# GpSimd's two-input work in parts of 192 columns, silu's low part on VectorE, and a list transposed one product group later

## The chip, the core and the metric

The kernel runs on one core of a Trainium2 chip. The core has five engines with a queue each: TensorE (PE; its weight loads are shown as PEld), VectorE (DVE), ScalarE (ACT), GpSimd (POOL) and SyncE (SP), which here only starts transfers. Each engine works through its own instructions in the order of the program and waits at semaphores for the others. The metric is the device time of one execution in microseconds, the median of three runs.

## What is computed

Three stages follow each other: attention with a hash mask, a silu MLP over all tokens, and eight experts of which each token uses one or none.

```python
# attention: 2 batches, 8 heads, 768 tokens, 64 columns a head
q_bucket, k_bucket = bits of (q @ proj > 0), (k @ proj > 0)
scores = where(q_bucket == k_bucket, q @ k.T / 8, -1e9)
x = softmax(scores) @ v                          # 1536 tokens x 512
# MLP, 2048 wide
h = x @ w_in
x = (h * sigmoid(h)) @ w_out
# experts: E = 8, each 512 -> 1024 -> 512
do = x @ w_skip > 0
e  = argmax(x[do] @ w_gate);  g = softmax(...)[e]
out = x;  out[do] = x + g * (relu(x @ w1[e]) @ w2[e])
```

## The kernel before

Matmuls take operands rounded to a shorter format (F32R), so nearly every operand is kept in two parts: a high part, the rounded copy, and a low part, the operand less its high part. Three products (high by high, low by high, high by low) then stand for one. In the names, `whi` and `wlo` are the parts of a weight, `gh` and `gl` those of silu's output `g`, `xhi` and `xlo` those of the attention's output, `xTh` and `xTl` those of an expert's transposed tokens. High parts are mostly made by ScalarE's copy, low parts by a subtraction on VectorE or GpSimd.

**Attention** goes over eight head pairs, twelve steps each, 96 in all. A step is one head and 128 query tokens: TensorE makes the scores `S` (line 381), VectorE their maximum `mx` (391) and from it the pair `bs` of scale and bias, two columns wide (393), ScalarE the exponentials `P` (395), TensorE their transposes `T` (407), ScalarE and VectorE copy these to `PT` (410, 412), and TensorE multiplies them by `v` (`pv`, 421). For every six steps the row sums `sums` (six columns) get 1e-9 added and are inverted on VectorE (425, 426), transposed on TensorE (`rT`, 432) and sent through memory to come back as `rb`; `em_x` then has GpSimd multiply `x` by `rb` (453), copy it to `xhi` (454) and subtract to get `xlo` (455). Beside a pair's steps the next pair's operands are made by `prep_op`: on ScalarE `K` (309) and `Q` (312), on GpSimd a copy of `Q` (312), the low part of `K` (316), the low part of `Q` (320), a scaling of `raw` (303) and the mask `mb` (337). The tables `PRE` and `POST` give the step in which each of these is issued.

**The MLP** goes over three blocks of 512 tokens and, in each, over 16 product groups f of 128 hidden columns, n = 0 to 47 in all. `em_h(n)` multiplies by `w_in` (`ph`, line 606, twelve matmuls), ScalarE makes `g` (612) and `gh` (613), and the subtraction for `gl` stands on line 615. TensorE then does `em_out(n - 1)` (`o`, 651 or 642). The MLP's weights come as 64-bit floats and are put together by `convert(f)`: ScalarE scales the upper word into `u` (214), VectorE shifts the lower one into `mag` (215), joins both (219) and writes the weight `wraw` (223). They are split in `splitting` into `whi` (ScalarE, 249) and `wlo` (VectorE, 252). In block 0 the loop over n converts f = n + 2 for n = 2 to 13 and splits n + 1, so a weight is made one group ahead of its use; later blocks find all weights in memory. The loop sets the order on ScalarE: `whi` of n + 1, `u` twice for n + 2, then `g` and `gh` of n.

**The experts** run a plan written as a list: `h` is one piece of the first product (six matmuls, `eh`, 1048), `y` one piece of the second (`ey`, 1070), `x` the transposition of an expert's gathered tokens, `t` that of its hidden values (both `tr`, 1026), `fetch` the gathers for later experts. Tokens per expert come from a list `id_d` that GpSimd scatters to memory (780). Experts 0 and 1 have theirs from a quicker way; the list of the others is read back as `eidr` (1000, a transfer on ScalarE's queue), transposed on TensorE as `eT` (1124) and written to `eid` by VectorE (1125). The start of the plan is

```python
fetch 0; h 0,0,0; h 0,0,1; h 0,1,0; t 0,0; h 0,1,1; y 0,0; y 0,1; x 1; t 0,1
fetch 1; h 1,0,0; h 1,0,1; y 0,2; y 0,3; t 1,0; ...
```

and before the change the transposition `eT` follows `t 0,1`. Behind `eid` stand the gathers for experts 2 and 3. `gT`, the gate weights on their way to memory, is copied on line 991.

Of the kernel before, what the change touches and what calls it, by code (L numbers as in the profile page):

```python
# [9 lines left out]
F32 = mybir.dt.float32  # L10
# [5 lines left out]
ALU = mybir.AluOpType  # L16
# [3 lines left out]
P = 128  # L20
# [5 lines left out]
def kernel(  # L26
# [16 lines left out]
    nc = tc.nc  # L43
    B, H, D, S = qT.shape
    NTOK, DM = out.shape
    NF = mw.shape[0]
# [3 lines left out]
    HQ = S // 2  # L50
# [5 lines left out]
    NT = NTOK // P  # L56
# [51 lines left out]
    xlo = xp.tile([P, KD, NTOK], F32R, name="xlo")  # L108
# [56 lines left out]
    NEARLY, NRING, NMORE = 4, 12, 8  # L165
# [98 lines left out]
    def attention(hook):  # L264
# [31 lines left out]
        def own(hd):  # L296
            return slice(hd * D, (hd + 1) * D)

        def prep_op(i, hd, what, eng):

            ks, qs = raws[i]
            if what == "scale":
                eng.tensor_scalar(ks, ks, SC, None, op0=ALU.mult)
                return
            Q1, K1, Q2, K2 = ops[i]
            r, o = own(hd), own(1 - hd)
            if what in ("kh", "k2"):
                dst = K1[r, hd] if what == "kh" else K2[0:D, hd]
                nc.scalar.activation(dst, ks[r], AF.Copy, scale=1.0 if i else SC)  # L309
            elif what in ("qa", "qb"):  # L310
                dst = Q1[r if what == "qa" else o, hd]
                (nc.scalar.copy if eng is nc.scalar else eng.tensor_copy)(dst, qs[r])
            elif what == "kl":
                h = K1[r, hd].bitcast(F32)
                if i:
                    eng.tensor_tensor(K1[o, hd], ks[r], h, op=ALU.subtract)
                else:
                    eng.scalar_tensor_tensor(K1[o, hd], ks[r], SC, h, op0=ALU.mult, op1=ALU.subtract)
            else:
                eng.tensor_tensor(Q2[0:D, hd], qs[r], Q1[r, hd].bitcast(F32), op=ALU.subtract)  # L320

        def prep_proj(i):

# [124 lines left out]
        def em_x(u, x, rb, eng):  # L448
            i, qh = units[u]
            b, p = divmod(i, NP)  # L450
            t0 = b * S + qh * HQ
            hi = xhi[:, p, t0:t0 + HQ]
            eng.tensor_tensor(x, x, rb, op=ALU.mult)
            eng.tensor_copy(hi, x)
            eng.tensor_tensor(xlo[:, p, t0:t0 + HQ], x, hi.bitcast(F32), op=ALU.subtract)


        mxs = [mainp.tile([P, 2], F32, name=f"mx{j}", bufs=1) for j in range(4)]
# [18 lines left out]
        Q1, K1, Q2, K2 = ops[0]  # L477
# [12 lines left out]
        for j, ps in enumerate(direct):  # L490
            r, c = mrow[j], (c_m, c_m, c_q)[j]
            t = mainp.tile([P, HQ], F32, name="rb" if j < 2 else "x", bufs=2)
# [103 lines left out]
    def em_h(n):  # L596
        b, f = items[n]
        hi, lo = splt[n]
# [12 lines left out]
        for p_, (c0, c1) in zip(ph, cut):  # L611
            nc.scalar.activation(g[:, c0:c1], p_[:, 0:c1 - c0], AF.Silu)  # L612
            nc.scalar.copy(gh[:, c0:c1], g[:, c0:c1])  # L613

            (nc.gpsimd if NEARLY <= n + 2 < NF else nc.vector).tensor_tensor(  # L615
                gl[:, c0:c1], g[:, c0:c1], gh[:, c0:c1].bitcast(F32), op=ALU.subtract)
        gs[n] = (gh, gl)

    def save_x(t, x):
# [210 lines left out]
    with tc.manual_schedule():  # L830
# [157 lines left out]
        gp = ps_tile("gp", [P, 512], "O1")  # L988
        nc.tensor.transpose(gp[0:NT, 0:P], gat, ident)
        gT = sm.tile([NT, P], F32, name="gT", bufs=1)  # L990
        nc.vector.tensor_copy(gT, gp[0:NT, 0:P])
        nc.sync.dma_start(g_d[0:NTOK].rearrange("(t p) c -> t (p c)", p=P), gT)
        fill(3, True)
        fetch_g(0)
# [106 lines left out]
        for n, (what, e, *at) in enumerate(plan):  # L1101
# [17 lines left out]
                xTs[e] = parts(xgs[e], "xT")  # L1119
            if (what, e, *at) == ("y", 0, 0):  # L1120
                fetch_list()
            if (what, e, *at) == ("t", 0, 1):
                ps = psE.tile([P, KD, P], F32, tag="T", name="eT", bufs=3)
                nc.tensor.transpose(ps[:, 0, 0:NE - 2], eidr, ident[0:NE - 2, 0:NE - 2])
                nc.vector.tensor_copy(eid[:, 2:NE], ps[:, 0, 0:NE - 2])
                fetch_x(2)
                fetch_g(2)
                fetch_x(3)
# [103 lines left out]
```

## Time and profile before

| | us |
|---|---|
| median of three runs | 642.49 (642.1 to 644.87) |
| the profiled execution, its own time | 647.16 |
| its span, first to last instruction | 645.4 |
| TensorE busy in the span | 616.6 |
| VectorE busy | 498.1 |
| ScalarE busy | 402.3 |
| GpSimd busy | 198.8 |

The profile is of one execution. Its span lies 1.8 us under that execution's own time, and that execution took 4.7 us more than the median run. Durations are read from the span; a difference that is worked out from them is then put on the median. Attention fills the span up to some 245 us, the MLP up to 519, the routing up to 532, the experts the rest. Times in the rows are counted from the start of the span. An instruction's "idle before" is the time its engine did nothing ahead of it, with what ended that; a duration holds also what an engine stands once it has taken up an instruction.

### The profile page before, as it was taken

The page shows a single profiled execution, that of the slowest core. Times are in us where ns is not written, and L with a number is a line of the kernel's source. Part 1 is how long each engine was busy: PE and PEld are TensorE (multiplying, and loading weights), DVE is VectorE, ACT ScalarE, POOL GpSimd, SP SyncE. Part 2 cuts the span into 40 slices and gives each one's busy share as a digit, 9 for nine tenths or more (in the row PEclk, how much of TensorE's full clock was granted, in tenths as well). Part 3 has the DMA queues.
Part 4 walks back from the last instruction along what each step waited for, and adds up shares of the span by engine and source line. Part 5 has one row for each costly group of instructions (what it writes and reads, how often), then busy time and mean ns, then how long its engine had stood idle before and what let it go on. Part 6 is the DMA issues. An engine that isn't in the chain of part 4 may idle for free.

```text
span 645.4 us, 9381 instructions
## 1 busy us (share of the span) xinstructions
PE 616.6 (96%) x3239; PEld 464.2 (72%) x3239; DVE 498.1 (77%) x882; ACT 402.3 (62%) x649; POOL 198.8 (31%) x172
## 2 busy tenths in 40 slices
PE   8899999999999999999999999999999977999996
PEld 3666666666566765887778887888887755788885
DVE  5988888988888777799986776447775458799992
ACT  4978778787877793555654444343344455788881
POOL 5457466474846113333210000020000044323201
PEclk9999999999999999999999999999999999899998
DMA  3320413222110313455443000024232348999800
GB/s 106 115 92 26 152 46 111 93 64 91 28 38 26 123 47 111 144 197 192 163 150 132 1 1 1 0 38 159 99 97 99 125 139 248 402 406 406 325 12 27
DMA packets 28736, 77.93 MB, mean 121 GB/s; under 512 B 5584, under 2 KB 9362, under 8 KB 28558
## 3 DMA queue, kind: packets, MB, share of 16 engines
q1 hardware_dynamic: 26594, 73.56, 33.4%
q0 software_dynamic: 1936, 3.65, 1.6%
q8 instruction: 26, 0.43, 0.3%
q14 instruction: 24, 0.20, 0.1%
q10 hardware_dynamic: 156, 0.10, 0.1%
HBM read 67.65 MB, written 8.50 MB: 118 GB/s over the span
## 4 chain that ended last, share of the span: by engine, by line
PE 77%; DVE 9%; ACT 7%; DMA 3%; issue 2%; POOL 1%; POOLq 0%; DVEq 0%; ACTq 0%
PE ph L606 21%; PE o L651 13%; PE pv L421 8%; PE S L381 7%; PE o L642 7%; PE T L407 6%; PE eh L1048 6%; PE ey L1070 5%; ACT P L395 3%; DVE mx L391 3%; DVE PT L412 2%; DVE sums L425 1%; ACT K L309 1%; PE tr L1026 1%; DMA id_d<-tk,slot 1%
## 5 line engine op out<-in xcount | busy, mean ns | idle before, releaser
L252 DVE TENSOR_TENSOR wlo<-wraw,whi 128x1024 fp32r<-128x1024 f32 x100 | 119.7, 1221 | 14.6 <-ACT whi L249 13.6
L249 ACT CAST whi<-wraw 128x1024 fp32r<-128x1024 f32 x100 | 102.9, 1051 | 43.4 <-DVE wraw L223 27.7
L395 ACT ACTIVATE P<-S,bs 128x768 f32<-128x768 f32 x96 | 95.4, 993 | 32.5 <-DVE bs L393 30.4
L381 PE MATMUL S<-K,Q 88*128 88x384 f32 (+1 forms) x384 | 92.9, 363 | 7.2 <-ACT P L395 6.9
L612 ACT ACTIVATE g<-ph 128x512 f32<-128x512 f32 x48 | 28.6, 595 | 109.7 <-PE ph L606 96.3
L391 DVE TENSOR_REDUCE mx<-S 128x1 f32<-128x768 f32 x96 | 90.8, 946 | 5.0 <-PE S L381 2.4
L407 PEld LDWEIGHTS T<-ident,P 128*128 128x128 f32 x576 | 67.8, 140 | 34.8 <-ACT PT L410 17.7
L407 PE MATMUL T<-ident,P 128*128 128x128 f32 x576 | 89.9, 277 | 2.9 <-DVE PT L412 2.2
L381 PEld LDWEIGHTS S<-K,Q 88*128 88x128 f32 (+1 forms) x384 | 63.2, 191 | 16.8 <-ACT P L395 11.0
L615 DVE TENSOR_TENSOR gl<-g,gh 128x512 fp32r<-128x512 f32 x36 | 25.0, 695 | 63.5 <-ACT gh L613 63.5
L421 PE MATMUL pv<-PT,v 128*64 128x384 f32 x384 | 72.5, 499 | 0.0
L780 POOL DMA_INDIRECT id_d<-tk,slot x12 | 13.0, 1080 | 184.5 <-DVE pre L788 181.5
L412 DVE COPY PT<-T 128x384 f32<-128x384 f32 x85 | 47.0, 552 | 16.1 <-PE T L407 15.9
L410 ACT COPY PT<-T 128x384 f32<-128x384 f32 x107 | 50.3, 477 | 10.5 <-PE T L407 10.1
L606 PE MATMUL ph<-xhi,whi 128*128 128x512 f32 x192 | 53.9, 402 | 0.3
L606 PE MATMUL ph<-xlo,whi 128*128 128x512 f32 x192 | 52.2, 393 | 0.0
L606 PE MATMUL ph<-xhi,wlo 128*128 128x512 f32 x192 | 52.1, 393 | 0.0
L664 DVE CUSTOM_DVE_ANT_0 junk<-x,gwb 128x512 bf16<-128x512 f32 x72 | 45.4, 686 | 0.0
L606 PEld LDWEIGHTS ph<-xhi,whi 128*128 128x128 f32 x192 | 34.8, 188 | 10.4 <-ACT whi L249 2.8
L606 PEld LDWEIGHTS ph<-xlo,whi 128*128 128x128 f32 x192 | 36.1, 188 | 8.5
L606 PEld LDWEIGHTS ph<-xhi,wlo 128*128 128x128 f32 x192 | 36.1, 188 | 8.3
L421 PEld LDWEIGHTS pv<-PT,v 128*64 128x64 f32 x384 | 23.3, 136 | 25.5 <-issue 23.2
(178 smaller groups left out, 1119.7 us busy)
## 6 DMA issues: line engine op xcount, KB each, us to landing
wraw<-in_w_dram SPq DMA_DIRECT2D x64, 512.0 KB
w<-in_mw_dram SPq DMA_DIRECT2D x32, 512.0 KB
v<-in_vt_dram SPq DMA_DIRECT2D x8, 384.0 KB
rb<-r_d SPq DMA_DIRECT2D x32, 96.0 KB
out_dram<-x SPq DMA_DIRECT2D x12, 256.0 KB
x_d<-x SPq DMA_DIRECT2D x11, 256.0 KB
raw<-in_kT_dram SPq DMA_DIRECT2D x7, 384.0 KB
raw<-in_qT_dram SPq DMA_DIRECT2D x7, 384.0 KB
```

The costliest lines, as they stand in the source:

```text
L249: nc.scalar.copy(hi[:, sl], t[:, sl])
L252: eng.tensor_tensor(lo[:, sl], t[:, sl], hi[:, sl].bitcast(F32), op=ALU.subtract)
L381: nc.tensor.matmul(ps[:, c, 0:HQ], q_[0:n, hd, q0:q0 + P], k_[0:n, hd, c * HQ:(c + 1) * HQ], start=first, stop=not first)
L391: nc.vector.tensor_reduce(mx[:, 0:1], ps[:, :, 0:HQ], axis=AX.XY, op=ALU.max, negate=True)
L395: nc.scalar.activation(pt.rearrange("p (a b) -> p a b", a=2), ps[:, :, 0:HQ], AF.Exp, bias=bs_[:, 0:1], scale=bs_[:, 1:2], accum_out=st_su ...
L407: nc.tensor.transpose(ps[:, j], pt[:, k * P:(k + 1) * P], ident)
L410: nc.scalar.copy(dst, ps)
L412: nc.vector.tensor_copy(dst, ps)
L421: nc.tensor.matmul(st_pv[u][hd * D:(hd + 1) * D], vts[i][:, k, hd], st_PT[u][:, hd, k], start=(k == 0), stop=(k == KT - 1))
L606: nc.tensor.matmul(p_[:, 0:c1 - c0], w[:, k * P:(k + 1) * P], x[:, k, t0 * P + c0:t0 * P + c1], start=(q == 0), stop=(q == len(ops3) - 1))
L651: nc.tensor.matmul(acc[t], g[:, (t - t0) * P:(t - t0 + 1) * P], w[:, DM:PIECE], start=(f == 0 and q == 0), stop=(f == NF - 1 and q == 2))
L664: nc.vector.tensor_tensor_reduce(junk, xts[t], pools["gwb_t"][:, c], op0=ALU.mult, op1=ALU.add, scale=1.0, scalar=0.0, accum_out=L[:, t, c ...
```

## The change

Five edits:

- `prep_op` issues GpSimd's low parts of `K` (for pairs after the first) and `Q` in four parts of 192 columns instead of one of 768.
- `em_x` issues the product with `rb` and the low part `xlo` in two parts of 192 instead of one of 384. The copies, the scaling and the mask on GpSimd stay whole.
- `gl` of the twelve groups that were on GpSimd (n = 2 to 13) goes to VectorE, where the other 36 are.
- `eT`, the copy to `eid` and the gathers behind it come after `h 1,0,0` instead of `t 0,1`.
- `gT` is copied by ScalarE instead of VectorE.

```diff
@@ -296,6 +296,10 @@
+        def pieces(n):
+
+            return [slice(c, c + 192) for c in range(0, n, 192)]
+
         def prep_op(i, hd, what, eng):
 
             ks, qs = raws[i]
@@ -313,11 +317,13 @@
             elif what == "kl":
                 h = K1[r, hd].bitcast(F32)
                 if i:
-                    eng.tensor_tensor(K1[o, hd], ks[r], h, op=ALU.subtract)
+                    for c in pieces(S):
+                        eng.tensor_tensor(K1[o, hd, c], ks[r, c], h[:, c], op=ALU.subtract)
                 else:
                     eng.scalar_tensor_tensor(K1[o, hd], ks[r], SC, h, op0=ALU.mult, op1=ALU.subtract)
             else:
-                eng.tensor_tensor(Q2[0:D, hd], qs[r], Q1[r, hd].bitcast(F32), op=ALU.subtract)
+                for c in pieces(S):
+                    eng.tensor_tensor(Q2[0:D, hd, c], qs[r, c], Q1[r, hd, c].bitcast(F32), op=ALU.subtract)
@@ -450,9 +456,12 @@
             hi = xhi[:, p, t0:t0 + HQ]
-            eng.tensor_tensor(x, x, rb, op=ALU.mult)
+            for c in pieces(HQ):
+                eng.tensor_tensor(x[:, c], x[:, c], rb[:, c], op=ALU.mult)
             eng.tensor_copy(hi, x)
-            eng.tensor_tensor(xlo[:, p, t0:t0 + HQ], x, hi.bitcast(F32), op=ALU.subtract)
+            lo = xlo[:, p, t0:t0 + HQ]
+            for c in pieces(HQ):
+                eng.tensor_tensor(lo[:, c], x[:, c], hi[:, c].bitcast(F32), op=ALU.subtract)
@@ -611,9 +620,7 @@
             nc.scalar.copy(gh[:, c0:c1], g[:, c0:c1])
-
-            (nc.gpsimd if NEARLY <= n + 2 < NF else nc.vector).tensor_tensor(
-                gl[:, c0:c1], g[:, c0:c1], gh[:, c0:c1].bitcast(F32), op=ALU.subtract)
+            nc.vector.tensor_tensor(gl[:, c0:c1], g[:, c0:c1], gh[:, c0:c1].bitcast(F32), op=ALU.subtract)
@@ -988,7 +995,7 @@
         gT = sm.tile([NT, P], F32, name="gT", bufs=1)
-        nc.vector.tensor_copy(gT, gp[0:NT, 0:P])
+        nc.scalar.copy(gT, gp[0:NT, 0:P])
@@ -1119,7 +1126,7 @@
-            if (what, e, *at) == ("t", 0, 1):
+            if (what, e, *at) == ("h", 1, 0, 0):
                 ps = psE.tile([P, KD, P], F32, tag="T", name="eT", bufs=3)
```

On GpSimd in attention, where one pair's second operands, the scaling and `em_x` follow each other, this stood before:

```order
L316 TENSOR_TENSOR K_481<-raw,K_481 64x768
L320 TENSOR_TENSOR Q_482<-raw,Q_480 64x768
L303 TENSOR_SCALAR raw<-raw 128x768
L453 TENSOR_TENSOR x<-x,rb 128x384
L454 CAST xhi<-x 128x384
L455 TENSOR_TENSOR xlo<-x,xhi 128x384
```

and this stands now:

```order
L321 TENSOR_TENSOR K_499<-raw,K_499 64x192 x4
L326 TENSOR_TENSOR Q_500<-raw,Q_498 64x192 x4
L307 TENSOR_SCALAR raw<-raw 128x768
L460 TENSOR_TENSOR x<-x,rb 128x192 x2
L461 CAST xhi<-x 128x384
L464 TENSOR_TENSOR xlo<-x,xhi 128x192 x2
```

The order is the same; of a pair's instructions four (`K`, `Q`) became sixteen and four (`x`, `xlo`) became eight.

On VectorE in the MLP's block 0, one turn of the loop over n, before (`mag` from `u` is line 219, `mag` from a loaded `w` line 215):

```order
L252 TENSOR_TENSOR wlo<-wraw,whi 128x1024
L219 SCALAR_TENSOR_TENSOR mag<-u,mag 128x512 x2
L223 SCALAR_TENSOR_TENSOR wraw<-u,mag 128x512 x2
L215 TENSOR_SCALAR mag<-w_3132 128x512
L215 TENSOR_SCALAR mag<-w_3184 128x512
```

and now:

```order
L252 TENSOR_TENSOR wlo<-wraw,whi 128x1024
L623 TENSOR_TENSOR gl<-g,gh 128x512
L219 SCALAR_TENSOR_TENSOR mag<-u,mag 128x512 x2
L223 SCALAR_TENSOR_TENSOR wraw<-u,mag 128x512 x2
L215 TENSOR_SCALAR mag<-w_3202 128x512
L215 TENSOR_SCALAR mag<-w_3252 128x512
```

`gl` of group n now stands ahead of the four steps that make the weight of group n + 2. ScalarE's order in the same place is not changed by the edit:

```order
L249 CAST whi<-wraw 128x1024
L214 ACTIVATE u<-w_3238 128x512
L214 ACTIVATE u<-w_3288 128x512
L612 ACTIVATE g<-ph 128x512
L613 CAST gh<-g 128x512
L249 CAST whi<-wraw 128x1024
```

On TensorE at the end of `t 0,1`, before:

```order
L1026 MATMUL tr<-ident,xg 128x128 x4
L1026 MATMUL tr<-ident,hr 128x128 x4
L1124 MATMUL eT<-ident,eidr 128x6
L1048 MATMUL eh<-whi,xTh 128x512
L1048 MATMUL eh<-wlo,xTh 128x512
```

and now:

```order
L1033 MATMUL tr<-ident,xg 128x128 x4
L1033 MATMUL tr<-ident,hr 128x128 x4
L1055 MATMUL eh<-whi,xTh 128x512
L1055 MATMUL eh<-wlo,xTh 128x512
L1055 MATMUL eh<-whi,xTh 128x512
L1055 MATMUL eh<-wlo,xTh 128x512
L1055 MATMUL eh<-whi,xTl 128x512 x2
L1131 MATMUL eT<-ident,eidr 128x6
```

Six matmuls of expert 1's first piece moved ahead of `eT`; on VectorE one split of a weight moved ahead of the copy to `eid` with them.

## Rows read from the trace of the kernel before

**Rows 1.** Page, part 4: the chain that ended last, by engine.

```profile
PE 77%; DVE 9%; ACT 7%; DMA 3%; issue 2%; POOL 1%; POOLq 0%; DVEq 0%; ACTq 0%
```

**Rows 2.** Who waited for whom, whole span: us in total, times, longest.

```profile
PE rT L432 <- DVE sums L426: 2.6, 7, 1.0
...
PE T L407 <- DVE PT L412: 2.2, 6, 0.4
```

**Rows 3.** Timeline, 42 to 52 us: start us, us, instruction, [idle before].

```profile
45.03 1.81 POOL L320 TENSOR_TENSOR Q<-raw,Q 64x768 fp32r<-64x768 f32 x1 [0.50 <-ACT Q L312]
...
45.25 1.62 DVE L425 TENSOR_SCALAR sums<-sums 128x6 f32<-128x6 f32 x1
...
46.80 1.00 POOL L453 TENSOR_TENSOR x<-x,rb 128x384 f32<-128x384 f32 x1
...
47.96 0.42 DVE L393 SCALAR_TENSOR_TENSOR bs<-mx 128x2 f32<-128x2 f32 x1
```

**Rows 4.** By source line: count, ns least/median/most, first and last start.

```profile
L425 DVE TENSOR_SCALAR sums<-sums x16: 155/766/1633, 31.6 to 248.0; 128x6 f32<-128x6 f32 x16
...
L223 DVE SCALAR_TENSOR_TENSOR wraw<-u,mag x24: 680/1232/1790, 262.9 to 328.2; 128x512 int32<-128x512 int32 x24
...
L615 DVE TENSOR_TENSOR gl<-g,gh x36: 691/693/754, 247.3 to 514.4; 128x512 fp32r<-128x512 f32 x36
```

**Rows 5.** One pair's stretch: us, busy us of PE, PEld, DVE, ACT, POOL; clock.

```profile
103.33:132.68 29.35, 27.92 (x180) 19.07 (x178) 25.97 (x49) 23.16 (x44) 17.40 (x15) 1.00 0.24 81
```

**Rows 6.** Timeline, 115 to 120 us, the third idle place in a pair.

```profile
115.85 0.84 ACT L309 ACTIVATE K<-raw 64x768 fp32r<-64x768 f32 x1
...
117.85 0.98 PE L381 MATMUL S<-K,Q 128*128 128x384 f32 x4 [0.80 <-ACT P L395]
```

**Rows 7.** Timeline, 285 to 298 us: one turn of the MLP's block 0.

```profile
289.03 1.06 ACT L249 CAST whi<-wraw 128x1024 fp32r<-128x1024 f32 x1 [2.53 <-DVE wraw L223]
...
291.13 0.58 ACT L612 ACTIVATE g<-ph 128x512 f32<-128x512 f32 x1
291.27 1.29 DVE L219 SCALAR_TENSOR_TENSOR mag<-u,mag 128x512 int32<-128x512 int32 x2
...
291.74 0.62 ACT L613 CAST gh<-g 128x512 fp32r<-128x512 f32 x1
...
292.47 2.39 DVE L223 SCALAR_TENSOR_TENSOR wraw<-u,mag 128x512 int32<-128x512 int32 x2
292.50 1.81 POOL L615 TENSOR_TENSOR gl<-g,gh 128x512 fp32r<-128x512 f32 x1 [4.04 <-ACT gh L613]
...
294.89 1.06 ACT L249 CAST whi<-wraw 128x1024 fp32r<-128x1024 f32 x1 [2.53 <-DVE wraw L223]
```

**Rows 8.** Timeline, 252 to 285 us: `whi` and `ph` of f = 3.

```profile
259.43 1.05 ACT L249 CAST whi<-w 128x1024 fp32r<-128x1024 f32 x1 [4.11 <-POOL xlo L455]
...
262.90 1.10 PE L606 MATMUL ph<-xhi,whi 128*128 128x512 f32 x4
```

**Rows 9.** Timeline, 329 to 343 us: the start of `ph` of f = 15.

```profile
331.12 1.20 PE L606 MATMUL ph<-xhi,whi 128*128 128x512 f32 x4
```

**Rows 10.** Timeline, 539 to 556 us: the experts' start.

```profile
540.23 0.73 PE L1070 MATMUL ey<-whi,hT0l 128*128 128x512 f32 x2 [1.10 <-DVE hT0l L1020]
...
543.96 0.68 DVE L1020 TENSOR_TENSOR xTl<-tr,xTh 128x512 fp32r<-128x512 f32 x1
...
546.21 0.24 PE L1124 MATMUL eT<-ident,eidr 6*128 6x6 f32 x1 [2.98 <-DMA eidr<-id_d]
```

**Rows 11.** The stretch behind the list, columns as in rows 5.

```profile
545.79:552.61 6.82, 6.40 (x16) 5.05 (x17) 2.53 (x3) 1.69 (x3) 3.75 (x3) 0.50 1.04 400
```

**Rows 12.** The chain that ended last, pieces in time: start us, us, what.

```profile
347.93 2.80 PE ph L606 x12
350.73 2.75 PE o L651 x12
...
546.45 5.42 PE eh L1048 x12
```

## The prediction

> **What bounds the kernel now.** I read the page first. TensorE carries 77% of the chain that ended last [rows 1], so an edit on another engine counts only where TensorE stands still for it. The list of who waited for whom shows where that is. TensorE waited 2.6 us in seven places at `rT` for `sums` (the longest, 1.0 us, lies behind attention, so six places share 1.6) and 2.2 us in six places at a transpose for the VectorE copy `PT` [rows 2]. Both waits come once for each head pair, at the same step. The timeline of one such step tells why: GpSimd starts `Q` at 45.03 and runs it 1.81 us; VectorE starts `sums`, six columns wide, 0.22 us later and is done at 46.87, 0.03 us behind the end of `Q`. `bs`, two columns wide, takes 0.42 us at 47.96 [rows 3]. Over the kernel `sums` takes 155 ns at least and 1633 at most [rows 4]. So a VectorE instruction of that kind stands until the GpSimd instruction in front of it is over. The same is seen in the MLP: the two `wraw` steps take 2.39 us beside `gl` on GpSimd, where a single one takes 680 ns undisturbed [rows 4, 7].
>
> In the MLP TensorE needs 2.80 us for `ph` and 2.75 for `o`, 5.55 us a product group [rows 12]. For groups f = 4 to 15 a weight is put together on VectorE and ScalarE and split just in time: `whi` comes at 289.03 and the next at 294.89, 5.86 us apart [rows 7]. That ring is slower than TensorE, yet starts ahead: `ph` of f = 3 begins at 262.90 and of f = 15 at 331.12 [rows 8, 9], where twelve free groups would end at 262.90 + 12 x 5.55 = 329.50. So 1.6 us are lost to it before the change.
>
> In the experts TensorE stands still for 2.98 us, from 543.23 to 546.21, for the list `eidr` [rows 10], and from 545.79 to 552.61 its granted clock is the lower of the two levels: the twelve matmuls of `eh` behind the wait take 5.42 us where twelve of that shape take 2.80 [rows 11, 12].
>
> **Parts of 192 columns in attention.** 768 columns take 1.81 us and 384 take 1.00 [rows 3], so a column costs 2.11 ns and an instruction 0.19 us; a part of 192 costs 0.19 + 0.41 = 0.59 us (bounds: a quarter of 1.81, 0.45, if the fixed part overlaps, and 0.67 with a gap of 0.08). Four parts take 0.55 us more than one instruction, two parts 0.19 more. A pair has four of the one kind and four of the other, 3.0 us on GpSimd's 17.40 us of 29.35 [rows 5], so it is still idle for nine, and in the list of waits TensorE never waits for `Q` or `K`; I cost the longer chain at nothing. What VectorE gains: `sums` starts 0.22 us into `Q` and would wait for the first part alone, until 45.62, and end 1.2 us sooner; the reduction, `bs` and `PT` behind it on VectorE follow. Then `rT` and the transpose find their operands ready, and the two waits go: 1.6 + 2.2 = **3.8 us**. The third place in a pair where TensorE is idle, 0.80 us at `S` for `P` [rows 6], I leave: there `P` stands behind ScalarE's `K` (115.85 to 116.70 [rows 6]), not behind `bs`. Bounds: 2.2 if new collisions with the longer GpSimd chain take back 1.6, and 5.0 if a part of that third place goes too.
>
> Whether VectorE gets in between two parts is the open point. The trace has such a boundary: `x` starts at 46.80, before `Q` is over at 46.84, and `sums` is done at 46.87 all the same, while `x` takes its plain 1.00 us [rows 3]. [...]
>
> **Silu's low part on VectorE.** Removed: twelve `gl` on GpSimd and with them the 1.1 us that they add to one `wraw` pair. Added: twelve of 0.69 us on VectorE [rows 4]. As work this is a gain for VectorE, but the order decides. `gl` now stands between `wlo` and the `mag` and `wraw` steps, and it waits for `gh`. `gh` stands on ScalarE behind the next `whi`, two `u` and `g`; that `whi` waited for the `wraw` before. So a ring closes that was open while GpSimd had `gl`: `whi`, `u`, `u`, `g`, `gh`, `gl`, `mag` twice, `wraw` twice, `whi`. Its length from one turn [rows 7]: 3.33 us from the start of `whi` at 289.03 to the end of `gh` at 292.36; handover 0.03 (as from `wraw` to `whi`); `gl` 0.69 less 0.09 overlap with the next on VectorE; from the first `mag` to the first `wraw` 1.20; the `wraw` pair undisturbed like the `mag` pair 1.29; handover 0.03. Sum 6.5 us, against 5.86 now and 5.55 on TensorE. Queued behind the waiting `gl` are the steps of the next weight; `whi`, and so TensorE, waits for them.
>
> The ring has twelve turns, from `whi` of f = 3 at 259.43 [rows 8] to that of f = 15: 259.43 + 78.0 = 337.4. That first `whi` waits for GpSimd's last `xlo` [rows 8], whose chain is now in parts; two more fixed costs of 0.19 lie ahead of it, partly beside VectorE work: 0.2 us. With 1.06 for `whi` and 0.05 handover `ph` of f = 15 starts at 338.7 instead of 331.12: **7.6 us** later. What is ahead of TensorE at the start (some 2.4 us) is used up by f = 6. From f = 16 weights are ready in memory and TensorE goes at 5.55 again without gaining back. Bounds: 6.4 us for a turn of 6.4, 9.2 for one of 6.6 and twice the delay at the start.
>
> **The list one group later.** In front of `eT` TensorE now has the six matmuls of `eh` 1,0,0. They start when `xTh` is ready (before 543.96, where `xTl` starts) and end behind `xTl` (544.64) [rows 10] with two matmuls more, at 545.1. The list still lands at 546.2: its scatter, its transfer and their queues are not moved. So the wait shrinks from 3.0 to 1.1 us, and behind it six matmuls are left instead of twelve. At full clock these end at 546.21 + 0.17 + 1.40 = 547.8; before, twelve ended at 551.87 and the rest of the slow stretch (0.74 us at half speed) cost 0.4 more. Gain **4.4 us**. It rests on the clock staying up: up to 545.8 TensorE was idle for 2.6 us at a stretch, now for 0.2 and 0.7. If it falls as before, six matmuls take 2.7 and end at 549.1; the gain is 2.8 us there less 1.4 in the groups behind, 1.4. Behind this the gathers for experts 2 and 3 start as before, `whi` waits for TensorE to give a buffer back and not for a transfer, and TensorE bounds the rest, so the gain stays. `gT` on ScalarE instead of VectorE: both stand idle there, nothing.
>
> **Sum.** -3.8 + 7.6 - 4.4 = -0.6 us. The profiled execution took 647.16 (span 645.4), so its like would take 646.6; the median of the three runs is 642.49, so I forecast **641.9 us**: no change that can be measured (0.5%, that is 3.2 us, is about what a measurement of this kernel can tell).
>
> **Rivals.** First: the clock falls at the list anyway. Then -3.8 + 7.6 - 1.4 = +2.4, 644.9. For it: TensorE still has a wait of about 1.1 us there. Against it: the wait of 1.10 us ahead of `ey` at 540.23 [rows 10] brought no fall.
>
> Second, the slower side: VectorE isn't let in between parts. Then `sums` waits for four parts, 2.36 less 0.22, 2.1 us instead of 1.6, and six waits grow by 0.5 each while none goes: +3.1 + 7.6 - 4.4 = +6.3, **648.8**. It decides from the point where GpSimd's parts follow each other without a break. Against it is the boundary in [rows 3].
>
> Third: the ring in the MLP doesn't bind, because `gh` is early. Then its 7.6 us don't come, and the 1.6 of now go: -3.8 - 1.6 - 4.4 = -9.8, 632.7. For it: VectorE is rid of 1.1 us of waiting a group and has 0.69 of work for it. Against it: the rows of one turn, in which each step follows the one before within 0.1 us.
>
> Fourth: the third idle place goes too, 0.8 us in four pairs: -3.8, 638.7. Against it is ScalarE's own work there.
>
> **How the numbers follow.** Forecast 0.68, first rival 0.13, second 0.07, third 0.06, fourth 0.06. The forecast's ends come from the bounds of its three terms, which won't all fall on one side: about 3 us either way. The range of 638.8 to 646.0 holds the forecast and the first rival and leaves out the second and third and half of the fourth. Faster by over 0.5% (under 639.3): third rival, half of the fourth, a tail of the forecast: 0.11. Slower by over 0.5% (over 645.7): the second, a part of the first and a tail: 0.15. Within: 0.74.
>
> **What would show it.** Right: `sums` nowhere above 0.8 us and no waits of `rT` for it in attention; `whi` of f = 5 to 15 spaced by 6.5 us, each behind a `wraw`, TensorE idle for 0.9 us before each `ph`, and 75.8 us from `ph` of f = 3 to f = 15; one wait of about 1.1 us at `eT` and full clock through 560. Wrong: a spacing of 5.6 in the MLP, `sums` of over 2 us, half clock behind `eT`, or TensorE waiting for `Q` or `K` of a pair in attention.

## The result: 650.03 us, slower by 1.1%

The changed kernel takes 650.03 us in the median of four executions (647.71 to 650.98) beside 642.3 of the kernel before, also of four (the 642.49 given ahead is the median of the first three). The ratio is 1.0107 with a 95% interval of 1.0069 to 1.0145, 4.4 to 9.3 us. The forecast was 641.9 with a range of 638.8 to 646.0: too low by 8 us, and on the wrong side.

The profiled execution took 650.98 us, span 649.1. The page of it, part 4, the chain that ended last by engine: TensorE's share, 77% in [rows 1], is now 67%, so the chain runs through other engines more than it did.

```profile
PE 67%; DVE 12%; ACT 12%; issue 4%; DMA 2%; POOL 1%; SPq 0%; POOLq 0%; DVEq 0%; ACTq 0%
```

Who waited for whom in it (us in total, times, longest), to be read beside [rows 2]:

```profile
ACT whi L249 <- DVE wraw L223: 38.1, 12, 3.2
...
PE ph L615 <- ACT whi L249: 6.9, 10, 0.8
...
PE T L413 <- DVE PT L418: 3.0, 6, 0.5
```

TensorE's waits at `rT` in attention are gone from the list (the one behind attention is left), but those at the transpose behind them grew from 2.2 to 3.0 us. And the matmuls of `ph` wait ten times for `whi`, a row that the list of before does not have.

Where the time went is plainest by stages. This table is worked out from the traces of all kernels of this study: the start of `S` of step 1 from the span's start; from there to `ph` of f = 0 (attention); to `ph` of f = 3; to f = 15; to the transposition `gp` at the end of the routing; and to the span's end (experts). All in us. The other labels are the experiments below; `c_before` is a second execution of the kernel before.

```
kernel      start attention  f0-f3  f3-f15   to gp experts
before      16.30    226.71  19.88   68.22  199.41  114.87
c_before    12.57    226.51  19.88   69.01  199.37  110.76
after       15.72    226.49  20.28   75.96  198.91  111.73
gl_only     16.05    226.68  19.88   75.57  199.71  110.70
parts_only  12.69    226.36  20.30   68.79  199.59  110.75
list_only   14.44    226.61  19.88   68.41  199.63  109.67
gl_late     15.52    226.37  20.28   66.53  198.96  110.15
gl_pool4    15.70    226.46  19.88   66.54  198.86  111.48
no_add      15.77    222.27  19.68   68.64  199.08  112.89
q96         15.55    223.50  20.29   68.45  198.92  111.89
q128        12.11    220.74  20.27   68.31  198.96  110.44
swap_kq     14.41    222.48  20.29   68.31  198.90  110.55
x_later     12.70    221.10  20.21   68.55  199.82  111.04
best1       12.72    222.20  19.68   66.54  199.05  108.68
best2       15.59    221.41  19.68   66.54  199.18  109.12
mended      11.81    221.32  20.28   66.54  199.80  113.09
best3       15.59    220.49  19.88   66.54  199.40  110.22
```

In three lines: attention did not get faster (226.49 beside 226.71 and 226.51), the MLP's block 0 got 7 to 8 us slower, and the experts gained 3.1 us against the one execution of before that the prediction read, but lost 1.0 against another of the same kernel (`c_before`).

**Attention.** Timeline of the changed kernel at the same step as [rows 3], two pairs on:

```profile
102.23 2.23 POOL L326 TENSOR_TENSOR Q<-raw,Q 64x192 fp32r<-64x192 f32 x4 [0.30 <-ACT Q L316]
102.46 1.50 DVE L431 TENSOR_SCALAR sums<-sums 128x6 f32<-128x6 f32 x1
...
104.44 1.14 POOL L460 TENSOR_TENSOR x<-x,rb 128x192 f32<-128x192 f32 x2
105.05 0.55 DVE L399 SCALAR_TENSOR_TENSOR bs<-mx 128x2 f32<-128x2 f32 x1
```

Four parts end at 102.82, 103.37, 103.92 and 104.47 by their single records. `sums` starts in the first and ends at 103.96, 0.03 us behind the third. So it stands 1.50 us where it stood 1.62, and the 0.12 us that it gains are lost at `bs`, which now meets the second part of `x`, where it met the copy `xhi`, and takes 0.55 us instead of 0.42 [rows 3]. A pair takes what it took [rows 5], though GpSimd works 2.3 us more:

```profile
124.47:153.83 29.36, 27.93 (x181) 19.07 (x180) 25.64 (x48) 23.15 (x43) 19.73 (x30) 1.00 0.26 80
```

**The MLP's block 0.** Timeline of one turn, to be read beside [rows 7]:

```profile
285.44 1.05 ACT L249 CAST whi<-wraw 128x1024 fp32r<-128x1024 f32 x1 [3.17 <-DVE wraw L223]
...
287.52 0.58 ACT L621 ACTIVATE g<-ph 128x512 f32<-128x512 f32 x1
...
288.13 0.62 ACT L622 CAST gh<-g 128x512 fp32r<-128x512 f32 x1
...
288.78 0.69 DVE L623 TENSOR_TENSOR gl<-g,gh 128x512 fp32r<-128x512 f32 x1 [1.04 <-ACT gh L622]
289.39 1.29 DVE L219 SCALAR_TENSOR_TENSOR mag<-u,mag 128x512 int32<-128x512 int32 x2
290.60 1.29 DVE L223 SCALAR_TENSOR_TENSOR wraw<-u,mag 128x512 int32<-128x512 int32 x2
...
291.92 1.05 ACT L249 CAST whi<-wraw 128x1024 fp32r<-128x1024 f32 x1 [3.17 <-DVE wraw L223]
...
293.02 1.20 PE L615 MATMUL ph<-xhi,whi 128*128 128x512 f32 x4 [0.77 <-ACT whi L249]
```

`wraw` no longer stands beside GpSimd: 1.29 us for two instead of 2.39. Yet VectorE is idle for 1.04 us ahead of `gl`, with the steps of the next weight queued behind it, and `whi` comes 6.48 us after `whi` instead of 5.86.

**The experts.** The granted clock fell here too, only earlier: at 538.50, while TensorE waited 1.28 us for the gathered tokens ahead of the experts' first matmuls, and not at the list. Windows of the changed kernel, columns as in [rows 5]; the clock is the third number from the end, 0.50 in the first and 1.00 in the second:

```profile
538.50:545.33 6.83, 6.38 (x16) 4.84 (x17) 5.21 (x6) 1.79 (x3) 3.58 (x7) 0.50 0.95 248
545.33:552.60 7.27, 7.04 (x37) 5.65 (x35) 6.59 (x8) 6.08 (x9) 2.13 (x3) 1.00 0.66 189
```

At `eT` itself nothing waits any more, where 2.98 us were lost in [rows 10]:

```profile
554.21 0.22 PE L1131 MATMUL eT<-ident,eidr 6*128 6x6 f32 x1
```

### The profile page after: what moved, and what is told of

Same layout as the page of the kernel before. It is cut to its first block, busy times and chain, and to the rows that moved or that the text cites. A ratio compares the mean times of both kernels' runs of the same rounds, so it can differ in the third digit from the quotient of the medians.

```text
span 649.1 us, 9472 instructions
## 1 busy us (share of the span) xinstructions
PE 617.3 (95%) x3239; PEld 463.6 (71%) x3239; DVE 489.1 (75%) x893; ACT 402.3 (62%) x650; POOL 197.1 (30%) x282
## 4 chain that ended last, share of the span: by engine, by line
PE 67%; DVE 12%; ACT 12%; issue 4%; DMA 2%; POOL 1%; SPq 0%; POOLq 0%; DVEq 0%; ACTq 0%
PE ph L615 15%; PE o L658 8%; PE pv L427 7%; PE S L387 7%; PE eh L1055 7%; PE o L649 7%; PE T L413 7%; PE ey L1077 6%; ACT P L401 3%; ACT u L214 3%; DVE mag L219 2%; DVE mx L397 2%; DVE PT L418 2%; DVE wraw L223 1%; PE tr L1033 1%
## 5 line engine op out<-in xcount | busy, mean ns | idle before, releaser
L252 DVE TENSOR_TENSOR wlo<-wraw,whi 128x1024 fp32r<-128x1024 f32 x100 | 119.8, 1222 | 11.4 <-ACT whi L249 10.3
L623 DVE TENSOR_TENSOR gl<-g,gh 128x512 fp32r<-128x512 f32 x48 | 33.7, 702 | 76.5 <-ACT gh L622 76.5
L387 PEld LDWEIGHTS S<-K,Q 88*128 88x128 f32 (+1 forms) x384 | 63.1, 191 | 16.1 <-ACT P L401 10.5
L321 POOL TENSOR_TENSOR K<-raw,K 64x192 fp32r<-64x192 f32 x56 | 31.7, 595 | 41.4 <-ACT K L313 35.4
```

What stands on the lines that cost most here:

```text
L252: eng.tensor_tensor(lo[:, sl], t[:, sl], hi[:, sl].bitcast(F32), op=ALU.subtract)
L387: nc.tensor.matmul(ps[:, c, 0:HQ], q_[0:n, hd, q0:q0 + P], k_[0:n, hd, c * HQ:(c + 1) * HQ], start=first, stop=not first)
```

## Experiments

Theories at the start: the ring through `gh` and `gl` is the whole loss (A), against a loss by VectorE's added work wherever it stands (B); the parts give nothing because VectorE is let in late (C), against a gain hidden by something else (D); the list's 4.4 us were mostly the clock of one execution (E), against a gain that is given back (F).

### The kernel before once more, and each edit alone

`c_before` is the kernel before, unchanged. `gl_only` moves the subtraction of the twelve groups and nothing else:

```diff
-            (nc.gpsimd if NEARLY <= n + 2 < NF else nc.vector).tensor_tensor(
-                gl[:, c0:c1], g[:, c0:c1], gh[:, c0:c1].bitcast(F32), op=ALU.subtract)
+            nc.vector.tensor_tensor(gl[:, c0:c1], g[:, c0:c1], gh[:, c0:c1].bitcast(F32), op=ALU.subtract)
```

`parts_only` is the change's edits in `prep_op` and `em_x`; `list_only` its last two, the place of `eT` and the copy `gT`.

> The kernel before, once more and unchanged. The question is whether the execution that was profiled (647.16 us, 4.7 over the median) stands for the others. Theory: it does not; the stretch at the lower clock behind the list (545.79 to 552.61) was its own. Then most executions here come near 642.3 with a mean granted clock near 0.999, and a profile without that stretch shows twelve matmuls of eh in 2.8 us behind the list instead of 5.42. Rival: the stretch belongs to the kernel and the profiler adds the rest; then the clock is 0.992 in every execution and a new profile shows the fall at the same place.

> Of the five edits only silu's low part on VectorE. Theory (the ring of whi, u, g, gh, gl, mag, wraw): whi of f = 5 to 15 is spaced 6.5 us, ph of f = 15 starts 7.6 us later counted from that of f = 3, and the kernel takes 642.3 + 7.6 = 649.9, nearly all that the whole change cost. Rival: the ring costs this only together with the parts, which delay its start; then this edit alone costs under 5 us, below 647.3.

> Of the five edits only GpSimd's subtractions and products in parts of 192 columns. Theory, from the trace of the changed kernel: sums still stands until the third of the four parts of Q is over, and bs behind it then meets a part of x, so a pair keeps its 29.35 us and the time stays within 1 us of 642.3. Rival, as the prediction had it: in that trace something else held the pairs back, and alone the parts give 3.8 us, 638.5.

> Of the five edits only the list's transposition one product group later, with gT copied by ScalarE. Theory: ordinary executions of before keep the full clock at the list, so that only the wait itself shrinks, by the 1.4 us of the six matmuls that now come first: 640.9. Rival one, the prediction: 4.4 us are gained, 637.9. Rival two: the transfers behind the list come later by as much and the gain is given back, 642.3.

Measured on one chip: before 641.34 (638.9 to 644.9); `c_before` 641.62; `gl_only` 650.10, ratio 1.0116 (1.0081 to 1.0151); `parts_only` 640.12, ratio 0.997 (0.995 to 0.999); `list_only` 641.06, ratio 0.9994 (0.9969 to 1.002).

`c_before`, profiled at 639.89 us, starts 3.7 us earlier than the profiled execution of [rows 1 to 12], waits 1.55 us for the list where that waited 2.98, and keeps the full clock behind it. Its timeline, its chain and its window at the list, beside [rows 10], [rows 12] and [rows 11]:

```profile
541.88 0.19 PE L1124 MATMUL eT<-ident,eidr 6*128 6x6 f32 x1 [1.55 <-DMA eidr<-id_d]
```

```profile
542.07 2.97 PE eh L1048 x12
```

```profile
541.88:548.70 6.82, 6.82 (x32) 5.65 (x33) 4.53 (x5) 4.03 (x6) 3.78 (x3) 1.00 1.04 412
```

So the span of 645.4 us held 8.1 that this second execution of the same kernel does not have: 3.7 at the start, 1.4 in the wait, 2.5 in the twelve matmuls and some 0.4 behind them; against that `c_before` lost 0.8 in the MLP's block 0. That is E. It is not the only execution with such a fall, though. Of the ten traces in which `eT` follows `t 0,1`, the clock falls behind the list in the two that waited longest for it, that of [rows 10] (2.98 us) and `no_add` (2.80 us); the other eight keep the full clock there. Of the seven with `eT` one group later none falls there, and three (`after`, `gl_late`, `mended`) fall at the experts' first matmuls instead.

The 3.7 us at the start look like the clock too. The same two matmuls of `S`, first in the profiled execution of before, then in `c_before`:

```profile
12.32 1.09 PE L381 MATMUL S<-K,Q 88*128 88x384 f32 x2
```

```profile
9.07 0.58 PE L381 MATMUL S<-K,Q 88*128 88x384 f32 x2
```

The traces have no record of the granted clock from there, so that it was lower is an estimate from the two durations: 1.09 us in the first, nearly twice the 0.58 of the second. The first granted clock that a trace records, the full one, stands at 12.6 to 13.5 us in nine traces, and their step 1 starts at 15.5 to 16.3; at 10.3 and 10.5 in two, which start at 14.4; and at 4.0 to 5.7 in the other six, which start at 11.8 to 12.7. Kernels with and without the parts stand in the first group and in the last. So the column `start` is no measure of an edit, and the edits are read from the columns behind it.

The list's edit is worth 1.1 us by the stages (109.67 beside 110.76), under what the times can tell: 641.06 fits the theory, 640.9, and also a gain that is given back, 642.3 (F). Only the 637.9 of the prediction is excluded.

`gl_only` costs what the whole change cost, 8.8 us by the medians, and its stretch takes 75.57, 7.4 and 6.6 more than in the two traces of before; the rival of a delay that needs the parts falls. The parts alone leave attention at 226.36. Their median is 0.3% lower, which no stage of the trace shows; since the start of an execution varies by more (11.81 to 16.30 us in the table), whether the edit has to do with it stays open.

### Where `gl` stands, not who does it

`gl_late` is the changed kernel with `gl` behind the next weight's steps: `em_h` no longer issues the subtraction but hands it back as `low`, to be called later. `gl_pool4` is the kernel before with `gl` on GpSimd in parts. Both excerpts leave out the lines that only follow from these.

```diff
-                if n >= len(EARLY_H):
-                    em_h(n)
+                low = em_h(n) if n >= len(EARLY_H) else None
                 for _ in cv:
                     pass
+                if low:
+                    low()
```

```diff
+            eng, size = (nc.gpsimd, 128) if NEARLY <= n + 2 < NF else (nc.vector, c1 - c0)
+            for c in range(c0, c1, size):
+                eng.tensor_tensor(gl[:, c:c + size], g[:, c:c + size], ...
```

> The changed kernel with one thing moved: in block 0 VectorE does gl of group n behind the four steps that make the weight of group n + 2, not ahead of them. Theory (the ring through gh and gl is what cost 7 us): the ring opens, a turn on VectorE is gl 0.69, two shifts 0.81, wlo 1.22, mag 1.29 and wraw 1.29, 5.3 us, under TensorE's 5.55; ph of f = 15 starts 66.6 us behind that of f = 3 (before 68.2 and 69.0, the changed kernel 75.96), and the time falls by 8 to 9 us against the changed kernel, to about 641. Rival: VectorE's added work itself is the bound, whatever its place; then the turn stays over 6 us and the stretch over 72.

> The kernel before with gl left on GpSimd in block 0, in four parts of 128 columns. Theory: VectorE's wraw gets in at the first boundary, waits 0.45 us instead of 1.1, a turn falls from 5.86 under 5.6, and ph of f = 15 starts 66.6 to 67.3 us behind that of f = 3 (before 68.2 and 69.0). Rival, as sums did in the changed kernel: VectorE stands until the third part is over; then a pair of wraw takes as long as now, 2.4 us, and the stretch stays at 68 to 69.

`gl_late` took 639.20 beside 642.54, ratio 0.9941 (0.9908 to 0.9975); its stretch is 66.53 us, TensorE's own twelve groups. B falls: the same work on the same engine, four instructions further on, gives back 9.4 us of the stretch (75.96 to 66.53). A turn of it, in which `gl` fills the time in which `whi` is made:

```profile
290.89 1.22 DVE L252 TENSOR_TENSOR wlo<-wraw,whi 128x1024 fp32r<-128x1024 f32 x1
292.03 1.29 DVE L219 SCALAR_TENSOR_TENSOR mag<-u,mag 128x512 int32<-128x512 int32 x2
293.23 1.29 DVE L223 SCALAR_TENSOR_TENSOR wraw<-u,mag 128x512 int32<-128x512 int32 x2
...
294.43 0.69 DVE L627 TENSOR_TENSOR gl<-g,gh 128x512 fp32r<-128x512 f32 x1
294.55 1.06 ACT L249 CAST whi<-wraw 128x1024 fp32r<-128x1024 f32 x1 [0.44 <-DVE wraw L223]
```

`gl_pool4` took 640.67, ratio 0.9973 (0.9949 to 0.9997), and its stretch 66.54: here VectorE is let in at the boundaries between parts. By source line (count, ns least/median/most):

```profile
L616 POOL TENSOR_TENSOR gl<-g,gh x48: 457/903/1037, 262.0 to 324.0; 128x128 fp32r<-128x128 f32 x48
...
L223 DVE SCALAR_TENSOR_TENSOR wraw<-u,mag x24: 678/946/958, 262.0 to 322.4; 128x512 int32<-128x512 int32 x24
```

A `wraw` stands 0.27 us over its 0.68 and no longer 1.1, and a part of 0.46 us mostly takes 0.90: GpSimd stands for VectorE too.

### What the wait at `sums` is worth, and when VectorE is let in

`no_add` takes the instruction `sums` away; the other four are `parts_only` with one more edit each: `q96` and `q128` have another size for `Q`'s low part (96 is shown, `q128` has 128 in its place), `swap_kq` exchanges `kl` and `ql` of the first head in `POST`, `x_later` issues `em_x` one step later.

```diff
-            nc.vector.tensor_scalar(st_sum[u], st_sum[u], 1e-9, None, op0=ALU.add)
```

```diff
-                for c in pieces(S):
+                for c in [slice(c, c + 96) for c in range(0, S, 96)]:
```

```diff
-        POST = [..., (3, 0, "kl", nc.gpsimd), (4, 0, "ql", nc.gpsimd), ...
+        POST = [..., (3, 0, "ql", nc.gpsimd), (4, 0, "kl", nc.gpsimd), ...
```

```diff
-                if k == 3 and u:
+                if k == 4 and u:
```

> The kernel before without the step sums that adds 1e-9 to the row sums (this addition is left out). Theory, the prediction's worth of the wait: sums standing 1.6 us beside GpSimd's Q is what makes TensorE wait at rT and at a transpose in six places; without it both waits go and a pair takes 28.7 us instead of 29.35, from S of step 25 to ph of the MLP's first group 113.24 falls by 2 us and the whole by 3 to 4. Rival: bs behind it only comes to wait beside the same Q, or the exponentials' chain sets the pair's time; then the pair stays at 29.3.

> Only the parts, but Q's low part in eight of 96 columns (about 0.39 us each, 0.35 apart). The question is what VectorE waits for at sums. If it is let in behind the second instruction after the one that it met (the third of four in the changed kernel), sums ends 1.1 us behind Q's start and takes 0.9 us. If it is let in only after a time (1.5 us in the changed kernel), sums takes 1.5 again. If it is let in one instruction before the last, it takes 2.5 or more. The pair's time stays near 29.35 in the last two, and may fall by 0.3 in the first.

> Only the parts, but Q's low part in six of 128 columns (about 0.46 us each, 0.42 apart). With parts of 192 sums was let in behind the third part, with parts of 96 behind the first, and there bs behind the eighth. If the size decides, sums takes between 0.2 (behind the first) and 1.1 us (behind the third). If only a request that falls on a boundary gets in, the one here falls 0.05 to 0.15 us ahead of one and waits for more than one part. The pair's time follows: 29.35 where sums and bs together stand over 1.9 us, under 29 where they stand under 1.4.

> Only the parts of 192, with GpSimd doing the first head's Q ahead of its K, so that sums meets parts of K (read on one half of the partitions, written on the other) where it met parts of Q (read and written on the same half). If the instruction decides, sums is let in behind the first part, as bs was at every K so far, and stands 0.3 us; the pair falls under 29. If the moment in the step decides, sums stands 1.4 us as with Q and the pair keeps 29.35.

> Only the parts of 192, and GpSimd's x, xhi and xlo come one step later, so that behind the first head's Q the mask mb follows, which has to wait for its operand, in place of x, which is ready. Nothing ahead of Q is changed. If what follows on GpSimd decides when VectorE gets in (with K behind Q it was the first boundary, with x the third), sums is let in behind the first part and stands 0.4 us; the pair falls under 29. If something ahead of Q decides, sums stands 1.4 to 1.5 us again, and only bs behind it, which no longer meets x, is let in at once; the pair falls to about 28.9 by that alone.

`no_add`: 638.72 beside 642.54, ratio 0.994 (0.9913 to 0.9967). Attention falls by 4.2 us and a pair to 28.8 (window of one pair, columns as in [rows 5]):

```profile
151.30:180.12 28.82, 27.54 (x181) 19.12 (x180) 25.13 (x47) 23.05 (x43) 17.36 (x14) 1.00 0.21 64
```

In its list of who waited for whom the row of `PT` is gone and of the seven waits at `rT` one is left, the one behind attention:

```profile
PE rT L431 <- DVE sums L425: 0.8, 1, 0.8
```

So the price that the prediction put on the wait, 3.8 us, was about right, though the edit takes away more than the six waits: the instruction itself and its shorter stands of 0.6 to 0.8 us in the second half of each pair. D falls, and what failed is the claim that parts of 192 remove the wait.

The other four are read by the stages of their traces. `q96` took 640.44, `q128` 632.68, `swap_kq` 636.71 and `x_later` 635.60, each a single time with a start of its own. In `q96` `sums` is let in behind the first part and takes 0.15 to 0.20 us, none of the three cases written down for it; then `bs` meets the fifth and is let in behind the seventh here, and in five other pairs only behind the last, after 1.25 to 1.34 us:

```profile
101.46 2.81 POOL L326 TENSOR_TENSOR Q<-raw,Q 64x96 fp32r<-64x96 f32 x8 [0.30 <-ACT Q L316]
101.68 0.19 DVE L431 TENSOR_SCALAR sums<-sums 128x6 f32<-128x6 f32 x1
...
102.96 1.04 DVE L399 SCALAR_TENSOR_TENSOR bs<-mx 128x2 f32<-128x2 f32 x1
```

`q128`: `sums` is let in behind the first part, `bs` behind the fifth, having met the fourth 0.12 us before its end. Attention falls by 5.8 us:

```profile
96.70 2.53 POOL L326 TENSOR_TENSOR Q<-raw,Q 64x128 fp32r<-64x128 f32 x6 [0.28 <-ACT Q L316]
96.92 0.27 DVE L431 TENSOR_SCALAR sums<-sums 128x6 f32<-128x6 f32 x1
...
98.27 0.56 DVE L399 SCALAR_TENSOR_TENSOR bs<-mx 128x2 f32<-128x2 f32 x1
```

Size alone does not explain it, for in `swap_kq` the parts are of 192 again, `sums` comes 0.22 us into the first as in the changed kernel, and is let in behind it, six times of six:

```profile
99.29 2.24 POOL L326 TENSOR_TENSOR Q<-raw,Q 64x192 fp32r<-64x192 f32 x4 [8.54 <-ACT Q L316]
99.51 0.40 DVE L431 TENSOR_SCALAR sums<-sums 128x6 f32<-128x6 f32 x1
...
101.00 0.55 DVE L399 SCALAR_TENSOR_TENSOR bs<-mx 128x2 f32<-128x2 f32 x1
```

The expectation was that `sums` would meet parts of `K` here; it met `Q` again, so the question whether the instruction decides was not put. But that kernel changes what runs ahead of `Q` and what follows it, which is now `K`. `x_later` changes only what follows: not `x`, which in the changed kernel is ready and starts 0.03 us before the last part ends, but `mb`, 3 us later:

```profile
125.80 2.25 POOL L326 TENSOR_TENSOR Q<-raw,Q 64x192 fp32r<-64x192 f32 x4 [0.34 <-ACT Q L316]
126.02 0.40 DVE L431 TENSOR_SCALAR sums<-sums 128x6 f32<-128x6 f32 x1
...
131.02 1.25 POOL L343 TENSOR_SCALAR mb<-ma,ct 128x384 fp32r<-128x384 f32 x1 [2.96 <-issue]
```

`sums` is let in behind the part that it meets in all six pairs (the first in five, the second in one), and attention falls by 5.4 us, some of it because `bs` no longer meets `x`. So with parts of 192 what stands behind them in GpSimd's queue decides when VectorE gets in: `sums` was held six times of six with `x` there, and never with `K` or `mb`.

`x` follows the parts in `q96` and `q128` too, where `sums` was not held. What the traces show beside that is how far ahead `x` was. Where `sums` passed two boundaries, and where `bs` did in `q96`, `x` was the fourth instruction behind the part that was met; where `bs` passed one in `q128`, the third; where `sums` was not held, the sixth and the eighth. Read so, it is a ready `x` close behind the part, and not `x` at any distance, that holds VectorE. This was found afterwards, and no run moves the distance alone. It is no full rule either: in `best2` below `bs` meets a part with `x` fifth behind it and is held in two pairs of six, and in `mended` `bs` once passes two boundaries between parts of `K` with no `x` near (at 17.51 us). How it comes about stays open.

### Together

`best1` is the kernel before with `no_add`, `gl_pool4` and `list_only`; `best2` adds `K` in parts of 192 and `Q` of 96; `best3` keeps `sums`, with `K` in 192 and `Q` in 128; `mended` is the changed kernel, all five edits, with `gl_late` and `Q` in 128.

> The kernel before with three things that paid in the earlier runs: no step sums (the addition of 1e-9 to row sums of at least 1 is left out), gl on GpSimd in four parts of 128 columns, the list one product group later. Theory: each works in its own stage and they add up; by the stages of the traces attention loses 4.2 us, the stretch from ph of f = 3 to f = 15 loses 2, the list 1.4: about 7.5 under before, 635 beside 642.5. Rival: what is gained ahead is lost to weights or transfers that come later; then it stays over 638.7, the time of the kernel without sums alone.

> As the one with the three things, and besides K and Q in parts (K 192, Q 96 columns), x and xlo whole. Without sums, bs is what meets GpSimd's Q. Theory: it is let in behind one part and waits 0.3 us instead of 0.6, and the pairs lose another 0.2 to 0.4 us each, 1 to 2 us less than its sibling. Rival: as bs did beside the eight parts (up to 1.2 us behind four of them), it is not let in at each boundary, and the parts give nothing or cost up to 2 us.

> The changed kernel, all five edits, with two sizes mended: Q's low part in six parts of 128 columns instead of four of 192, and gl on VectorE behind the steps of the next weight. Theory: by the stages attention loses 5.8 us against before, the stretch to ph of f = 15 loses 2 and its start gains 0.4, the list 1.4; about 8.5 under before. Rival: the gains meet each other and are given back at the start of the experts, where the list's transfer is no earlier than before; then under 6.

> Nothing left out: K in parts of 192, Q in parts of 128, x and xlo whole, gl on GpSimd in four parts of 128, the list one product group later. Theory: attention as with Q in parts of 128 alone (5.8 us less than before), no later start of the MLP's block 0, the stretch to f = 15 at 66.5, the list 1.4: 9.3 under before, like or better than the kernel without sums and with Q in parts of 96. Rival: x whole holds bs for up to 1 us in each pair, and attention gains 3 us less.

`best1` 631.14 beside 639.89, ratio 0.9864 (0.983 to 0.9898); `best2` 629.67 beside the same, 0.9836 (0.9802 to 0.987); `mended` 633.66 beside 642.95, 0.9847 (0.9813 to 0.9882); `best3` 632.40 beside 642.95, 0.9836 (0.9805 to 0.9867). The gains of the stages add up, and none is given back: 8.7 us were measured for `best1`, where 7.5 were summed, 9.3 for `mended`, where 8.5 were, and 10.6 for `best3`, where 9.3 were. `best2` is 1.5 us better than its sibling, as hoped, but the two intervals overlap, and attention differs by 0.8 us in the traces. All four beat both kernels; `best3` does so with nothing left out, and the intended change does so too (`mended`) once the size of `Q`'s parts and the place of `gl` are mended.

## Why the prediction was wrong, step by step

- **The MLP's term was right.** Forecast: a ring of 6.5 us a turn, 0.2 us later at its start, 75.8 us from f = 3 to f = 15, 7.6 us in all. Measured: 6.48, 0.40, 75.96, and 7.4 and 8.1 us by the two traces of before. The step that found it was to write down who is queued behind the added wait; `gl_late` confirms it by taking that queue away. TensorE stood 0.6 to 0.8 us ahead of each `ph`, where 0.9 was written. The third rival, a ring that does not bind, falls.
- **Attention's term failed**: 3.8 us were forecast, none came. The step is the sentence that `sums` "would wait for the first part alone, until 45.62". It rested on one boundary of the trace, that of two instructions of different kinds, `Q` and `x`, and was taken for a rule of every boundary. The second rival named the case on the other side, VectorE not let in between parts; what happened lies between the two: let in at the third boundary of three, six times. That rival's price, 3.1 us more, did not come either, since three parts are as long as the old wait. The price of the wait itself was about right (`no_add`, 4.2, with the rest of `sums` in it), also the cost of a part (0.59 us). The lower bound of 2.2 was too high: a new collision, of `bs` with `x`, took back the little that `sums` gained.
- **The experts' term was mis-sized**: 4.4 us forecast, 1.1 measured by the stages (`list_only`). The step is that a clock which fell in this execution was put to the kernel's account: 2.6 us of the matmuls and 0.4 behind them. `c_before` keeps the full clock there, as seven of the other eight traces with the list in its old place do, so there was mostly nothing to get back. The prediction said that its profiled execution lay 4.7 us over the median, and then moved the difference to the median as if each term held there too. The first rival asked only whether the clock would fall behind the change; whether it falls without it was not asked. In the changed kernel it fell at another place, at 538.50, against the forecast of a full clock through 560. At `eT` nothing was waited for, where 1.1 us had been forecast.
- **`gT` and GpSimd's longer chain** cost nothing that shows: TensorE waits nowhere for `Q` or `K` of a pair, though GpSimd works 2.3 us more in each (3.0 forecast).

With the terms as measured against `c_before` the sum is 0.0 for attention, +7.4 for the MLP's block 0, -0.5 up to `gp` and +1.0 for the experts, 7.8 us; the medians differ by 7.7. That the two agree so well is luck in part: the start, 3.2 us later in this trace, is left out, and each side is one execution. The last +1.0 is the fall of the clock, and the later gathered tokens ahead of it, less the list's gain. Why those tokens came later is not settled: the first `eh` starts 2.70 us behind `gp`, 1.0 to 1.7 in most traces, 2.1 in `gl_late` and `q96`. (`mended` has 3.6, but there the tokens were transposed at once, and ScalarE copied them late.)

## What to carry to other kernels

Before an operation is moved to another engine, write down what is queued behind it there: here the move took work and waiting off both engines and cost 7 us, because it waited in front of the work that feeds the next turn, and placed behind that work it gave 2 us. Where two engines stand for each other, one may be let in at a boundary, but one boundary in a trace is a sample, not a rule; where the gain hangs on it, try two or three sizes. And a time that sits in one profiled execution, a slow clock or a late start above all, is to be looked for in a second one before it is put into a sum.

## What the runs showed of the hardware

- VectorE's small steps (`sums`, `bs`) that meet back-to-back GpSimd parts are mostly let in at the end of the part that they met (within 0.03 us of it), but not always. `sums` passed two boundaries beside parts of 192 in six pairs of six (1.39 to 1.50 us), and `bs` passed three beside parts of 96 in five pairs of six (1.25 to 1.34 us) and one beside parts of 128 in six of six (0.56 us). Each time a ready `x` stood third or fourth behind the part that was met, and exchanging what follows the parts ended the hold (0.18 to 0.40 us in `x_later`). A `bs` that came 0.03 to 0.05 us before the boundary of two parts of 192 was let in at the next one (0.60 to 0.62 us).
- It works both ways: GpSimd's parts of 128 columns took 0.46 us at least and 0.90 in the median beside VectorE's `wraw`.
- The time to the first steps of attention goes from 11.81 to 16.30 us in the table, and by 3.7 us between two executions of the same kernel, more than most edits here are worth; it goes with the time at which the full clock is first recorded, 4.0 to 13.5 us. Stages counted from one named instruction to another agree better in these two executions: within 0.2 us in attention, 0.8 in the MLP's block 0; the experts, with the fall of the clock in one of them, differ by 4.1.
